# Joined high and low operands in the last group of a two-layer kernel's split products

## The chip, the core and the metric

The kernel runs on one core of a Trainium2 chip. The metric is the device time of one execution in microseconds (us), of which three runs were taken. TensorE (PE) multiplies, VectorE (DVE) and ScalarE (ACT) work on the operands and results, GpSimd (POOL) helps at the start, and SyncE (SP) issues the transfers (DMAs) one after the other.

## The reference

Sigmoid attention feeds a two-layer network with a squared ReLU:

```python
scores = scale * np.matmul(q, k.transpose(0, 1, 3, 2)) - np.log(S)
attn_out = np.matmul(1.0 / (1.0 + np.exp(-scores)), v)
x = np.ascontiguousarray(attn_out.transpose(0, 2, 1, 3)).reshape(B * S, H * D)
h = x @ w_in
r = np.maximum(h, 0.0)
return ((r * r) @ w_out).astype(np.float32)
```

q, k and v are 8 × 12 × 448 × 64, so x has 3584 rows (tokens) and 768 columns; w_in is 768 × 2048 and w_out 2048 × 768. All is float32.

## The kernel before

The kernel computes attention first and then the two weight products in four groups of tokens, `GROUPS = ((0, 512), (1024, 512), (2048, 512), (3072, 256))`. A group (g = 0 to 3) is two blocks of T tokens, so the last, g = 3, has T = 256 where the others have 512. Only this last group concerns us.

**Seven products.** Each of the two matrix products is cut in 2 × 2 blocks and computed by a scheme of Strassen's kind: 7 products of blocks, named 1 to 7, from sums and differences of operand blocks, and sums of the results. **High and low parts.** Each operand is split in a high part (the value cast to fp32r, by ScalarE, L349) and a low part (the rest, a subtraction on VectorE, L351), and each product is three matmuls: high·high, high·low, low·high (`product`, L561). A matmul has 128 rows of weights and T columns.

**First product** (`gemm1`, L569). i runs over 8 slices of the hidden columns. A step (n, i) is product n for slice i: 3 slices of the contraction times 3 matmuls, 9 in all. The steps run in a list: (1,i), (5,i−1), (2,i), (6,i), (3,i−1), (7,i), (4,i−1). Products 1, 6, 5 and 3 accumulate in PSUM bank `ha`, 7 and 4 in `hb`, 2 in `hc`. After 1, 6 and 5 ScalarE copies the bank (`snap`, L607: tiles s1, s2, s4, L609), and TensorE goes on accumulating in it only after that: (6,i) waits for s1, (5,i) for s2, (3,i) for s4. VectorE adds banks and snaps to the blocks g11, g22, g21 (L627, L633, L642), and ScalarE makes g12 from the bank (L636, Relu). j counts pairs of i; when a pair is complete, `squares` makes relu(h)² of 512 columns at once, on VectorE for 11, 22 and 21 (L592), on ScalarE for 12 (L590).

**Weights of the first product** come in four kinds: w1A (products 1 and 2), w1B (6 and 7), w1C (5 and 3), w1D (4). `load_weights` (L228) takes a buffer of a pool of 7 wide ones, shared with the weights w2 of the second product, and the load waits until TensorE is done with the buffer's last user. SP issues all loads in one order, so a load that waits holds back those behind it.

**Order.** Most steps of `gemm1` are ordered by a scheduler when the program is built. The last ten, (1,7), (5,6), (2,7), (6,7), (3,6), (7,7), (5,7), (4,6), (3,7), (4,7), with the first loads of the second product, run under `manual_schedule` (L666 to L683) in the order in which they are written. The list `work` says behind which of the ten a load (`load`, `load_last`), a split (`halve`) or an operand stands.

**Second product** (`gemm2`, L687): order 1, 2, 6, 7, 5, 4, 3; for each product 4 values of j, with one w2 tile `w2_3_n_j` and one operand each, both split, and 72 matmuls. While product n runs, the operands and weights of the next are prepared. Results are in banks oa, ob, oc; `snap` (L734) copies, `put` (L718) adds on VectorE or copies on ScalarE, and a DMA writes the output.

## Time and profile before

| | us |
|---|---|
| median of three runs | 1058.42 |
| lowest and highest run | 1058.36 and 1059.52 |
| profiled execution | 1058.8 |
| its span (first to last instruction) | 1057.0 |
| last group, first product | 59.96 |
| last group, second product | 61.78 |

The profile is of one execution, whose own time is 1058.8 us; 1.8 us lie around its span. Times in the views are from the start of the span. PE is TensorE's matmuls and PEld its weight loads, which overlap. A row of matmuls names the bank, the operand and the weights with buffer numbers left out, so `ha<-xht,w1C` is a matmul of some (5,i) or (3,i). A duration of one matmul is longer than the distance to the next, since they overlap.

### The profile page before, as it was taken

To read this page: it belongs to the slowest core of one execution; us is meant where nothing else is said; L and a number is where in the kernel's file an instruction comes from. 1 tells how busy PE (TensorE), PEld (TensorE's weight loads), DVE (VectorE), ACT (ScalarE), POOL (GpSimd) and SP (SyncE) were. 2 spreads that over 40 slices of the span, in tenths; PEclk is the share of its full clock that TensorE was granted. 3 is DMA by queue.
4 is the path that set the end of the run, shared out by engine and by line. 5 is a ranking of instruction groups with operands and counts; after the bars stand their busy time and mean duration, and the time that the engine had idled before them with its cause. 6 is when DMAs were issued, how large, how long until landed. Compare 5 with 4: busy or idle time off the path is not lost.

```text
span 1057.0 us, 16721 instructions
## 1 busy us (share of the span) xinstructions
PE 1052.7 (100%) x6433; PEld 825.5 (78%) x6433; DVE 798.7 (76%) x1009; ACT 650.8 (62%) x910; POOL 72.4 (7%) x42
## 2 busy tenths in 40 slices
PE   9999999999999999999999999999999999999998
PEld 4555555557888888888888888888888888899998
DVE  5999999996776699854555899655555998457896
ACT  7989999986766765534333757244334765255763
POOL 1322232210121000000000000000000000000000
PEclk9999999999999999999999999999999999999999
DMA  9988999964665335544332446443334344456664
GB/s 355 394 301 313 378 396 330 364 236 139 198 214 162 105 112 192 172 125 117 100 88 87 118 131 209 144 136 89 90 103 112 105 150 134 150 162 195 190 201 123
DMA packets 90832, 196.13 MB, mean 186 GB/s; under 512 B 8320, under 2 KB 51712, under 8 KB 90752
## 3 DMA queue, kind: packets, MB, share of 16 engines
q1 hardware_dynamic: 90608, 195.00, 56.6%
q8 instruction: 50, 0.82, 0.3%
q14 instruction: 30, 0.25, 0.1%
q10 hardware_dynamic: 144, 0.07, 0.0%
HBM read 154.14 MB, written 40.89 MB: 185 GB/s over the span
## 4 chain that ended last, share of the span: by engine, by line
PE 99%; DMA 0%; ACT 0%; issue 0%; DVE 0%; ACTq 0%
PE oa L565 22%; PE ha L565 22%; PE ob L565 11%; PE hb L565 11%; PE pav L313 11%; PE sc L282 9%; PE oc L565 5%; PE hc L565 5%; PE sr L298 2%; PE pav L325 2%; DMA w1C<-w 0%; PE warm_ps L791 0%; ACT w1C L349 0%; ACT o L727 0%; ACT s L609 0%
## 5 line engine op out<-in xcount | busy, mean ns | idle before, releaser
L349 ACT CAST w<-w 128x768 fp32r<-128x768 f32 x112 | 92.5, 835 | 91.4 <-DMA w<-w 86.8
L351 DVE TENSOR_TENSOR w<-w 128x768 fp32r<-128x768 f32 x112 | 106.4, 952 | 26.7 <-ACT w L349 26.3
L270 ACT ACTIVATE at<-sc 128x896 f32<-128x896 f32 x144 | 119.3, 942 | 4.1 <-PE sc L282 4.1
L609 ACT COPY s<-ha 128x512 f32<-128x512 f32 (+1 forms) x96 | 51.0, 532 | 110.7 <-PE ha L565 106.8
L313 PE MATMUL pav<-at,v 64*64 64x448 f32 x1152 | 118.1, 540 | 0.0
L313 PEld LDWEIGHTS pav<-at,v 64*64 64x64 f32 x1152 | 41.9, 133 | 60.6 <-issue 53.6
L351 DVE TENSOR_TENSOR w1A<-w1A 128x768 fp32r<-128x768 f32 x31 | 29.7, 957 | 60.6 <-ACT w1A L349 59.4
L519 DVE TENSOR_TENSOR ql<-x,qh 128x896 fp32r<-128x896 f32 x47 | 72.4, 1580 | 0.0
L166 POOL TENSOR_TENSOR a<-a,f 128x768 int32<-128x768 int32 x26 | 58.2, 2238 | 160.1 <-DVE a L163 105.7
L565 PE MATMUL oa<-o_0h,w 128*128 128x512 f32 (+1 forms) x192 | 55.7, 362 | 0.0
L565 PE MATMUL oa<-o_1h,w 128*128 128x512 f32 (+1 forms) x192 | 55.5, 362 | 0.0
L565 PE MATMUL oa<-o_2h,w 128*128 128x512 f32 (+1 forms) x192 | 55.5, 362 | 0.0
L565 PE MATMUL oa<-o_3h,w 128*128 128x512 f32 (+1 forms) x192 | 55.5, 362 | 0.0
L349 ACT CAST w1A<-w1A 128x768 fp32r<-128x768 f32 x32 | 26.7, 834 | 45.1 <-DMA w1A<-w 45.1
L282 PE MATMUL sc<-qh 64*128 64x448 f32 x282 | 54.2, 380 | 0.0
L282 PE MATMUL sc<-ql,qh 64*128 64x448 f32 x282 | 51.6, 361 | 0.0
L282 PE MATMUL sc<-qh,ql 64*128 64x448 f32 x282 | 51.6, 361 | 0.0
L351 DVE TENSOR_TENSOR w1B<-w1B 128x768 fp32r<-128x768 f32 x31 | 30.6, 988 | 25.1 <-ACT w1B L349 25.1
L351 DVE TENSOR_TENSOR w1C<-w1C 128x768 fp32r<-128x768 f32 x32 | 30.7, 960 | 18.7 <-ACT w1C L349 18.6
L592 DVE SCALAR_TENSOR_TENSOR g<-g 128x1024 f32<-128x1024 f32 (+1 forms) x40 | 42.6, 1064 | 1.2
L349 ACT CAST w1B<-w1B 128x768 fp32r<-128x768 f32 x32 | 26.7, 835 | 25.5 <-DMA w1B<-w 25.1
L349 ACT CAST w1C<-w1C 128x768 fp32r<-128x768 f32 x32 | 26.7, 833 | 25.4 <-DMA w1C<-w 25.4
(189 smaller groups left out, 2815.6 us busy)
## 6 DMA issues: line engine op xcount, KB each, us to landing
w<-w SPq DMA_DIRECT2D x112, 384.0 KB, 3.4
x<-qk SPq DMA_DIRECT2D x47, 448.0 KB, 6.6
f<-w_in SPq DMA_DIRECT2D x16, 768.0 KB, 8.9
w1A<-w SPq DMA_DIRECT2D x32, 384.0 KB, 3.1
w1B<-w SPq DMA_DIRECT2D x32, 384.0 KB, 3.3
w1C<-w SPq DMA_DIRECT2D x32, 384.0 KB, 3.4
v<-v SPq DMA_DIRECT2D x24, 448.0 KB, 7.5
w<-s SPq DMA_DIRECT2D x26, 384.0 KB, 7.9
```

Of the source, the lines that this page charges most:

```text
L166: nc.gpsimd.tensor_tensor(out=wb, in0=wb, in1=t.bitcast(I32)[:, :, 0], op=ALU.add)
L270: nc.scalar.activation(at, sc, AF.Sigmoid, bias=NEG_LOG_S, scale=SCALE)
L282: nc.tensor.matmul(sc[:, j], x[kp][rows, 1, ks], x[qp][rows, 0], start=(n == 0), stop=(n == len(passes) - 1),)
L298: nc.tensor.matmul(sc[r * KR : (r + 1) * KR, j], x[rows, 1, NT * P :], x[rows, 0], start=True, stop=True)
L313: nc.tensor.matmul(sums[columns, h], vt[rows, n % 2 * NT + t, columns], at[t][rows, j], start=(t == 0 and (n % 2, h) != (1, 1)), stop=(t = ...
L325: nc.tensor.matmul(sums[r][columns, r], vt[rows, 2 * NT, columns], rest[rows, j], start=(r == 1), stop=(r == 0))
L349: nc.scalar.copy(out=hi, in_=raw)
L351: nc.vector.tensor_sub(out=lo, in0=raw, in1=hi.bitcast(F32))
L519: nc.vector.tensor_sub(out=xs[n][1], in0=x[n], in1=xs[n][0].bitcast(F32))
L565: nc.tensor.matmul(out, a[:, c], b, start=first and n == 0, stop=last and n == 2, skip_group_check=True)
L592: nc.vector.scalar_tensor_tensor(out=t, in0=t, scalar=0.0, in1=t, op0=ALU.max, op1=ALU.mult)
L609: nc.scalar.copy(out=s, in_=banks["a", i])
```

## The change

It touches the last group only (`joined` is set where 2T is at most 512).

- **Joined operands.** High and low part of an operand lie side by side in one tile (`operand_of`, and `make` for x). In products 2, 7 and 4 of the first and 6, 7, 5 and 4 of the second, high·high and high·low become one matmul of 512 columns over both, and low·high one of 256. The bank then holds two halves.
- **Sums.** `total` adds a half and a snap, then the other half: two VectorE adds of 256 columns instead of one. In the second product snaps 6 and 7 are 512 wide, a snap 5 is new, and the sums of 22 and 21 are one add of 512 and one of 256 columns. For 12, two VectorE adds of 128 columns stand in place of ScalarE's copies.
- **Shared buffers.** Blocks 11 and 12 share a tile (g1), 22 and 21 another (g2).
- **w1D** has buffers of its own (L243 of the kernel after), not of the wide pool.
- **First weights of the second product** (w2_3_1_j) have buffers of their own too, and are loaded and split among the steps of the first product (`early`).
- **Squares** of blocks 22 and 21 are by ScalarE (Relu, then Square), except the last pair's; they are issued at the end of the step that follows the block's last sum (`flush`).

```diff
     def load_w1(g, i, kind):
         ns = KINDS[kind]
         at = min(PLACE[0][n] for n in ns)
-        return load_weights(w1[i][:, at : at + len(ns)], f"w1{kind}_{g}_{i}")
+        name = f"w1{kind}_{g}_{i}"
+        src = w1[i][:, at : at + len(ns)]
+        if kind == "D" and g == NG - 1:
+            t = op2(name, F32R, NS)
+            hi, lo = t[:, 0:1, :HALF], t[:, 1:2, :HALF]
+            nc.sync.dma_start(out=lo.bitcast(F32), in_=src)
+            return hi, lo
+        return load_weights(src, name)
...
+            else:
+                x = op2(f"xj{n}_{g}", F32R, 2 * T)
+                kind, at = SPOT[product]
+                if kind not in ys:
+                    ys[kind] = op2(f"yj{kind}_{g}", F32R, 2 * T)
+                y = ys[kind][:, at]
+                (h2, l2), (h1, l1) = ((t[..., :T], t[..., T:]) for t in (x, y))
+                ops[product] = [(h2[:, c], l2[:, c], x[:, c]) for c in range(2)] + [(h1, l1, y)]
...
     def load_w2(g, n, j):
         blocks_of = w2.rearrange("i p n c -> n p i c")[PLACE[1][n]]
-        return load_weights(blocks_of[:, 2 * j : 2 * j + 2], f"w2_{g}_{n}_{j}")
+        src, name = blocks_of[:, 2 * j : 2 * j + 2], f"w2_{g}_{n}_{j}"
+        if g == NG - 1 and n == 1:
+            hi, lo = (op2(f"{name}{c}", F32R, NS)[:, :, :HALF] for c in "hl")
+            nc.sync.dma_start(out=lo.bitcast(F32), in_=src)
+            return hi, lo
+        return load_weights(src, name)
...
-    def product(out, w, c, x, first, last):
+    def product(out, w, c, x, first, last, both=None):
 
         (wh, wl), (xh, xl) = w, x
+        if both is not None:
+            nc.tensor.matmul(out, wh[:, c], both, start=first, stop=last, skip_group_check=True)
+            nc.tensor.matmul(
+                out[:, : xh.shape[-1]], wl[:, c], xh, start=False, stop=last, skip_group_check=True
+            )
+            return
...
+    def operand_of(g, raw, name):
+        T = GROUPS[g][1]
+        if 2 * T > NS:
+            return (*split(raw, name, lambda *names: op2(*names, T)), None)
+        both = op2(name, F32R, 2 * T)
+        hi, lo = both[:, :, :T], both[:, :, T:]
+        split_to(hi, lo, raw)
+        return hi, lo, both
+
...
+        joined = (2, 7, 4) if 2 * T <= NS else ()
...
+            j = i // 2
+            if (n, j) not in blocks:
+                if 2 * T > NS:
+                    blocks[n, j] = op2(f"g{n}_{g}_{j}", n=T)
+                else:
+                    t = op2(f"g{n[0]}_{g}_{j}", n=2 * T)
+                    for k, c in enumerate("12"):
+                        blocks[n[0] + c, j] = t[:, k].rearrange("p (a s) -> p a s", a=2)
+            return blocks[n, j][:, i % 2]
...
-            if g == 0:
+            if g == 0 or (g == NG - 1 and i < NI - 2):
                 pending.append(lambda: squares(n, i, scalar=True))
             else:
                 squares(n, i)
...
+        def total(to, from_, s):
+            nc.vector.tensor_add(out=to, in0=from_[:, :T], in1=s)
+            if joined:
+                nc.vector.tensor_add(out=to, in0=from_[:, T:], in1=to)
...
             for c in range(NE):
-                product(out, w, c, ops[n][c], n in (1, 7, 2) and c == 0, c == NE - 1)
+                *x, both = ops[n][c]
+                product(out, w, c, x, n in (1, 7, 2) and c == 0, c == NE - 1, both if n in joined else None)
...
-                nc.vector.tensor_add(out=tile_of("11", i), in0=out, in1=snaps[1, i])
+                total(tile_of("11", i), out, snaps[1, i])
...
-                nc.vector.tensor_add(out=tile_of("22", i), in0=banks["b", i], in1=snaps[4, i])
+                total(tile_of("22", i), banks["b", i], snaps[4, i])
                 squares_later("22", i)
...
-                nc.vector.tensor_add(out=tile_of("21", i), in0=out, in1=snaps[2, i])
+                total(tile_of("21", i), out, snaps[2, i])
                 squares_later("21", i)
...
-            operands[j] = split(blocks["11", j], f"o1_{g}_{j}", lambda *name: op2(*name, T))
+            operands[j] = operand_of(g, blocks["11", j], f"o1_{g}_{j}")
...
+        early = {}
+        if g == NG - 1:
+            for j in range(NI // 2):
+                early[30 + 3 * j] = lambda j=j: load(j)
+                early[35 + 3 * j] = lambda j=j: halve(j)
         for at, (n, i) in enumerate(head):
             run(n, i)
             for work in between.get(at, ()):
                 work()
+            if at in early:
+                early[at]()
...
+        work = [(at, piece, arg) for at, piece, arg in work if not (early and piece in (load, halve))]
...
+        joined = (6, 7, 5, 4) if 2 * T <= NS else ()
...
-            ops.setdefault(n, {})[j] = split(raw, f"o{n}_{g}_{j}", new)
+            ops.setdefault(n, {})[j] = operand_of(g, raw, f"o{n}_{g}_{j}")
...
-            if add is not None:
-                nc.vector.tensor_add(out=o, in0=banks[k, e], in1=snaps[add, e])
-            elif g == NG - 1 and e == NE - 1:
-
+            if name == "11":
+                nc.vector.tensor_add(out=o, in0=banks[k, e], in1=s)
+            elif joined and name == "12":
                 for columns, queue in ((slice(0, T // 2), nc.sync), (slice(T // 2, T), nc.scalar)):
-                    nc.scalar.copy(out=o[:, columns], in_=banks[k, e][:, columns])
-                    queue.dma_start(out=to[:, columns], in_=o[:, columns])
-                return
+                    nc.vector.tensor_add(out=o[:, columns], in0=banks[k, e][:, columns], in1=s[:, columns])
+                    if e == NE - 1:
+                        queue.dma_start(out=to[:, columns], in_=o[:, columns])
+                if e == NE - 1:
+                    return
+            elif joined:
+                nc.vector.tensor_add(out=s, in0=banks[k, e], in1=s)
+                nc.vector.tensor_add(out=o, in0=s[:, :T], in1=s[:, T:])
+            elif add is not None:
+                nc.vector.tensor_add(out=o, in0=banks[k, e], in1=s)
             else:
                 nc.scalar.copy(out=o, in_=banks[k, e])
             nc.sync.dma_start(out=to, in_=o)
...
-            s = snaps[n, e] = op1(f"t{n}_{g}_{e}", n=T)
-            nc.scalar.copy(out=s, in_=banks[k, e])
+            from_ = banks[k, e][:, {1: slice(T), 5: slice(T, 2 * T)}.get(n, slice(None))]
+            s = snaps[n, e] = op1(f"t{n}_{g}_{e}", n=from_.shape[-1])
+            nc.scalar.copy(out=s, in_=from_)
...
-                    banks[k, e] = bank(f"o{k}_{g}_{e}")[:, :T]
+                    banks[k, e] = bank(f"o{k}_{g}_{e}")[:, : (2 if joined and n != 2 else 1) * T]
...
-                        x = tuple(t[:, i % 2] for t in ops[n][j])
-                        product(banks[k, e], w, e, x, n in (1, 7, 2) and i == 0, i == NI - 1)
+                        x, both = tuple(t[:, i % 2] for t in ops[n][j][:2]), None
+                        to = banks[k, e][:, :T]
+                        if n in joined:
+                            both, to = ops[n][j][2][:, i % 2], banks[k, e]
+                        product(to, w, e, x, n in (1, 7, 2) and i == 0, i == NI - 1, both)
...
+                    if joined:
+                        snap(5, k, e)
                     put("22", e, 1, 7)
                 elif n == 3:
-                    put("12", e, 1, None)
+                    put("12", e, 1, 5 if joined else None)
```

**Where instructions move.** Names in these rows: `w1D_3_5` is the weights of kind D, group 3, i = 5, `s4_3_6` the snap after (5,6), `w2_3_2_2` the weights of product 2, j = 2, in the second product, `g2_3_2` the shared tile of blocks 22 and 21, j = 2 (i = 4 and 5); the last number counts tiles.

TensorE near the end of the first product, before: the last of (7,6), then (4,5), which is `hb_3_5` with w1D_3_5, then the first of (1,7).

```order
L565 MATMUL hb_3_6_8935<-xht3_3_8271,w1B_3_6_8908 128x256
L565 MATMUL hb_3_6_8935<-yt3_3_8273,w1B_3_6_8908 128x256 x3
L565 MATMUL hb_3_5_8838<-xht4_3_8407,w1D_3_5_8945 128x256
L565 MATMUL hb_3_5_8838<-xlt4_3_8408,w1D_3_5_8945 128x256
L565 MATMUL hb_3_5_8838<-xht4_3_8407,w1D_3_5_8945 128x256 x2
L565 MATMUL hb_3_5_8838<-xlt4_3_8408,w1D_3_5_8945 128x256
L565 MATMUL hb_3_5_8838<-xht4_3_8407,w1D_3_5_8945 128x256
L565 MATMUL hb_3_5_8838<-yt4_3_8409,w1D_3_5_8945 128x256 x3
L565 MATMUL ha_3_7_8978<-xh11_3_8137,w1A_3_7_8960 128x256
```

And after: the last of (2,7), then (6,7), (4,5) and the first of (3,6), which is `ha_3_6` with w1C_3_6.

```order
L588 MATMUL hc_3_7_8975<-yjA_3_8138,w1A_3_7_8927 128x256
L593 MATMUL ha_3_7_8945<-xjt2_3_8223,w1B_3_7_8935 128x256 x6
L593 MATMUL ha_3_7_8945<-yjB_3_8224,w1B_3_7_8935 128x256 x3
L587 MATMUL hb_3_5_8808<-xjt4_3_8394,w1D_3_5_8915 128x512
L588 MATMUL hb_3_5_8808<-xjt4_3_8394,w1D_3_5_8915 128x256
L587 MATMUL hb_3_5_8808<-xjt4_3_8394,w1D_3_5_8915 128x512
L588 MATMUL hb_3_5_8808<-xjt4_3_8394,w1D_3_5_8915 128x256
L587 MATMUL hb_3_5_8808<-yjD_3_8395,w1D_3_5_8915 128x512
L588 MATMUL hb_3_5_8808<-yjD_3_8395,w1D_3_5_8915 128x256
L593 MATMUL ha_3_6_8833<-xj22_3_8346,w1C_3_6_8931 128x256 x6
```

The step (4,5) has moved from behind (7,6) to behind (6,7), past (1,7), (5,6) and (2,7); (3,6) comes right after it.

SP at the same place, before: the loads from w1C of i = 5 on.

```order
L232 DMA w1C_3_5_8879<-w1 128x768
L232 DMA w1B_3_6_8908<-w1 128x768
L232 DMA w1D_3_5_8945<-w1 128x384
L232 DMA w1A_3_7_8960<-w1 128x768
L232 DMA w1C_3_6_8964<-w1 128x768
L232 DMA w1B_3_7_8968<-w1 128x768
L232 DMA w1D_3_6_8972<-w1 128x384
L232 DMA w1C_3_7_8990<-w1 128x768
```

And after, from w1C of i = 7 to the first weights of product 6.

```order
L232 DMA w1C_3_7_8959<-w1 128x768
L232 DMA w2_3_2_0_9081<-w2 128x2x384
L232 DMA w2_3_2_1_9106<-w2 128x2x384
L232 DMA w2_3_2_2_9131<-w2 128x2x384
L243 DMA w1D_3_5_8915<-w1 128x384
L243 DMA w1D_3_6_8939<-w1 128x384
L232 DMA w2_3_2_3_9156<-w2 128x2x384
L243 DMA w1D_3_7_8998<-w1 128x384
L232 DMA w2_3_6_0_9192<-w2 128x2x384
```

The loads w1D_3_5 and w1D_3_6 have moved behind the loads of w1C_3_7 and of w2_3_2_0 to w2_3_2_2, each of which waits for a wide buffer; w2_3_2_2 takes the one of w1B_3_6.

ScalarE at the same place, before: the snaps of (1,7), (5,6) and (6,7) and what follows.

```order
L609 COPY s1_3_7_8988<-ha_3_7_8978 128x256
L609 COPY s4_3_6_9001<-ha_3_6_8867 128x256
L609 COPY s2_3_7_9028<-ha_3_7_8978 128x256
L349 CAST w1C_3_7_8990<-w1C_3_7_8990 128x768
L636 ACTIVATE g12_3_3_9043<-ha_3_6_8867 128x256
L349 CAST w2_3_1_0_9017<-w2_3_1_0_9017 128x768
L609 COPY s4_3_7_9068<-ha_3_7_8978 128x256
```

And after, from the snap of (1,7) to that of (5,7).

```order
L653 COPY s1_3_7_8955<-ha_3_7_8945 128x256
L356 CAST w2_3_2_1_9106<-w2_3_2_1_9106 128x768
L356 CAST w2_3_2_2_9131<-w2_3_2_2_9131 128x768
L356 CAST w1D_3_5_8915<-w1D_3_5_8915 128x384
L356 CAST w1D_3_6_8939<-w1D_3_6_8939 128x384
L356 CAST w2_3_2_3_9156<-w2_3_2_3_9156 128x768
L633 ACTIVATE g2_3_2_8762<-g2_3_2_8762 128x512
L634 ACTIVATE g2_3_2_8762<-g2_3_2_8762 128x512
L653 COPY s4_3_6_8970<-ha_3_6_8833 128x256
L653 COPY s2_3_7_8994<-ha_3_7_8945 128x256
L356 CAST w1C_3_7_8959<-w1C_3_7_8959 128x768
L686 ACTIVATE g1_3_3_8872<-ha_3_6_8833 128x256
L356 CAST w2_3_6_0_9192<-w2_3_6_0_9192 128x768
L653 COPY s4_3_7_9026<-ha_3_7_8945 128x256
```

The snap s4_3_6 stood behind s1_3_7; now five casts of weights and the Relu and Square of g2_3_2 stand between them.

## Rows read from the trace of the kernel before

**Rows 1.** From the page: busy time (share of span) and count by engine; granted clock in 40 slices

```profile
PE 1052.7 (100%) x6433; PEld 825.5 (78%) x6433; DVE 798.7 (76%) x1009; ACT 650.8 (62%) x910; POOL 72.4 (7%) x42
...
PEclk9999999999999999999999999999999999999999
```

**Rows 2.** Busy by stretch (first, second product): us, PE, PEld, DVE, ACT, POOL, clock

```profile
932.22:992.18 59.96, 59.90 (x498) 59.69 (x497) 40.72 (x68) 33.81 (x68) 0.00 (x0) 1.00 0.61 183
992.18:1053.96 61.78, 61.77 (x513) 61.39 (x512) 52.90 (x81) 39.37 (x66) 0.00 (x0) 1.00 0.60 174
```

**Rows 3.** Waits of TensorE's queue, 925 to 1058: us in all, times, longest

```profile
PEld ha L565 <- ACT s L609: 0.3, 1, 0.3
PEld hb L565 <- DVE w1D L351: 0.2, 1, 0.2
```

**Rows 4.** The chain that ended last, 925 to 1058: start, us, what

```profile
958.38 4.19 DMA w1C<-w
...
962.65 0.83 ACT w1C L349
963.48 0.28 ACT s L609
```

**Rows 5.** Timeline of TensorE, 512 columns, the group ahead: start, us, instruction

```profile
924.28 0.39 PE L565 MATMUL oa<-o_2l,w 128*128 128x512 f32 x1
...
927.68 0.39 PE L565 MATMUL oa<-o_2l,w 128*128 128x512 f32 x1
```

**Rows 6.** Timeline of TensorE, 256 columns, first product of the last group

```profile
960.35 0.28 PE L565 MATMUL ha<-xht,w1C 128*128 128x256 f32 x1
...
962.51 0.28 PE L565 MATMUL ha<-xht,w1B 128*128 128x256 f32 x1
```

**Rows 7.** VectorE by line and form, 932.3 to 1054: count | busy us, mean ns | idle before

```profile
L351 DVE TENSOR_TENSOR w<-w 128x768 fp32r<-128x768 f32 x28 | 26.6, 951 | 1.3 <-ACT w L349 1.2
L592 DVE SCALAR_TENSOR_TENSOR g<-g 128x512 f32<-128x512 f32 x12 | 8.3, 688 | 0.2
...
L351 DVE TENSOR_TENSOR w1D<-w1D 128x384 fp32r<-128x384 f32 x7 | 3.9, 552 | 0.0
L642 DVE TENSOR_TENSOR g<-hb,s 128x256 f32<-128x256 f32 x8 | 3.4, 420 | 1.5 <-PE hb L565 1.5
```

**Rows 8.** ScalarE by line and form, 932.3 to 1054

```profile
L609 ACT COPY s<-ha 128x256 f32<-128x256 f32 x24 | 8.7, 369 | 5.9 <-PE ha L565 5.9
...
L349 ACT CAST w1D<-w1D 128x384 fp32r<-128x384 f32 x7 | 3.6, 509 | 0.0
...
L590 ACT ACTIVATE g<-g 128x512 f32<-128x512 f32 x4 | 2.5, 630 | 0.0
```

**Rows 9.** DMA issues, 930 to 1058: count, KB each, median us to landing

```profile
w<-w SPq DMA_DIRECT2D x28, 384.0 KB, 3.6
w1C<-w SPq DMA_DIRECT2D x7, 384.0 KB, 3.7
...
w1D<-w SPq DMA_DIRECT2D x7, 192.0 KB, 2.3
```

**Rows 10.** Timeline of SP's issues, 981 to 983

```profile
981.37 0.37 SPq L232 DMA_DIRECT2D w<-w  x1
982.45 0.32 SPq L232 DMA_DIRECT2D w1D<-w  x1
```

**Rows 11.** DMA issues of 981 to 982, 982 to 983, 985.6 to 986

```profile
w<-w SPq DMA_DIRECT2D x1, 384.0 KB, 3.9
...
w1D<-w SPq DMA_DIRECT2D x1, 192.0 KB, 3.2
...
w<-w SPq DMA_DIRECT2D x1, 384.0 KB, 3.1
```

**Rows 12.** Timeline of ScalarE, three casts in a row

```profile
995.15 2.30 ACT L349 CAST w<-w 128x768 fp32r<-128x768 f32 x3
```

**Rows 13.** End of the chain that ended last

```profile
1054.19 0.27 ACT o L727
```

More of the change, by code (lines that the diff above doesn't have):

```diff
@@ L379, in sub @@
                 nc.vector.tensor_sub(out=o, in0=x, in1=y)
-        ops = {}
+        ops, ys = {}, {}
         def make(product, n, later=None):
-            h2, l2, both = (op2(f"{c}{n}_{g}", F32R, T) for c in ("xh", "xl", "y"))
-            h1, l1 = both[:, 0], both[:, 1]
-            ops[product] = [(h2[:, 0], l2[:, 0]), (h2[:, 1], l2[:, 1]), (h1, l1)]
+            if 2 * T > NS:
+                y = op2(f"y{n}_{g}", F32R, T)
+                h1, l1 = y[:, 0], y[:, 1]
+                h2, l2 = (op2(f"{c}{n}_{g}", F32R, T) for c in ("xh", "xl"))
+                ops[product] = [(h2[:, c], l2[:, c], None) for c in range(2)] + [(h1, l1, None)]
+            else:
[6 more added lines that the diff above has]
+                ops[product] = [(h2[:, c], l2[:, c], x[:, c]) for c in range(2)] + [(h1, l1, y)]
             for x, (hi, lo) in zip(raw[n], [(h2, l2), (h1, l1)]):
@@ L578, in tile_of @@
         def tile_of(n, i):
-            if (n, i // 2) not in blocks:
-                blocks[n, i // 2] = op2(f"g{n}_{g}_{i // 2}", n=T)
-            return blocks[n, i // 2][:, i % 2]
+            j = i // 2
+            if (n, j) not in blocks:
+                if 2 * T > NS:
+                    blocks[n, j] = op2(f"g{n}_{g}_{j}", n=T)
[4 more added lines that the diff above has]
+            return blocks[n, j][:, i % 2]
         def squares(n, i, scalar=False):
@@ L617, in run @@
             if n in (1, 7, 2):
-                banks[k, i] = bank(f"h{k}_{g}_{i}")[:, :T]
+                banks[k, i] = bank(f"h{k}_{g}_{i}")[:, : (2 if n in joined else 1) * T]
             out = banks[k, i]
@@ L691, in gemm2 @@
         t2 = {}
-        def new(name, dtype):
-            return op2(name, dtype, T)
+        joined = (6, 7, 5, 4) if 2 * T <= NS else ()
         def operand(n, j):
@@ L698, in operand @@
                 if j not in operands1:
-                    operands1[j] = split(blocks["11", j], f"o1_{g}_{j}", new)
+                    operands1[j] = operand_of(g, blocks["11", j], f"o1_{g}_{j}")
                 if j not in weights1:
@@ L720, in put @@
             o = op1(f"o{name}_{g}_{e}", n=T)
+            s = snaps.get((add, e))
             to = outT[(r + e) * P : (r + e + 1) * P, t0 + b * T : t0 + (b + 1) * T]
-            if add is not None:
-                nc.vector.tensor_add(out=o, in0=banks[k, e], in1=snaps[add, e])
-            elif g == NG - 1 and e == NE - 1:
+            if name == "11":
+                nc.vector.tensor_add(out=o, in0=banks[k, e], in1=s)
+            elif joined and name == "12":
                 for columns, queue in ((slice(0, T // 2), nc.sync), (slice(T // 2, T), nc.scalar)):
-                    nc.scalar.copy(out=o[:, columns], in_=banks[k, e][:, columns])
-                    queue.dma_start(out=to[:, columns], in_=o[:, columns])
-                return
+                    nc.vector.tensor_add(out=o[:, columns], in0=banks[k, e][:, columns], in1=s[:, columns])
[8 more added lines that the diff above has]
+                nc.vector.tensor_add(out=o, in0=banks[k, e], in1=s)
             else:
```

## The prediction

> **What bounds the kernel now.** I read four views in this order. First, the page: TensorE is busy for all of the span at full clock, VectorE for 76% of it [rows 1]. So time can be won only by giving TensorE less to do, and is lost wherever TensorE has to wait. Second, the busy times of the two products of the last group, the only stretch that the change touches [rows 2]: the first product lasts 59.96 us, the second 61.78 us, together 121.74 us. They hold 1008 matmuls of 256 columns, and 1008 × 0.120 us (the pitch, below) is 120.96 us. TensorE hardly waits there, while VectorE has 19 us and 9 us free and ScalarE more. Third, the waits of TensorE's queue in the last group [rows 3]: two, 0.3 us for a ScalarE copy and 0.2 us for the low part of w1D. Fourth, the chain that ended last [rows 4], which shows how the first arises: a weight load (w1C) landed late, its cast stood ahead of the snap on ScalarE, and TensorE waited for the snap. That pattern, an instruction that waits for a transfer with a snap queued behind it, is the one to look for in the new order.
>
> **What the joining removes.** Three matmuls of 256 columns (high·high, high·low, low·high) become one of 512 and one of 256 columns. The columns stay the same; only one instruction's fixed part goes. From pitches: 15 matmuls of 512 columns start from 924.28 up to 927.68 [rows 5], so 3.40/15 = 0.2267 us; 18 of 256 columns from 960.35 up to 962.51 [rows 6], 2.16/18 = 0.120 us. Three of 0.120 are 0.360 us, one of each is 0.3467 us: 0.0133 us saved a triple. Per product of the first stage there are 3 such triples, 3 products and 8 values of i: 72. In the second, 4 products of 24 triples: 96. So 168 triples, 168 × 0.0133 = **2.24 us** gained, all on TensorE.
>
> The Trainium skill, page "TensorE: Matmul & The Clock Gate", section "Back-to-back issue gap", speaks against this: by its isolated gap of N/2.4 + 2.5 ns only 2.5 ns are fixed in a matmul, an estimate of 168 × 2.5 ns = 0.42 us for the gain, and a sum of 1064.4 below. The trace disagrees (227 ns at 512 columns where that formula gives 216, 120 at 256 where it gives 109) and decides.
>
> **What the joining adds** is work of VectorE, since the halves of a bank must be summed: 24 more adds of 256 columns in the first product, against 6 squares of 512 columns that go to ScalarE. By [rows 7], 24 × 0.42 − 6 × 0.69 = +5.9 us, to about 46.6 of 60 us. In the second, the end sums get a few adds longer and the 4 splits of the first weights (4 × 0.95) move ahead, so its 52.9 us hardly change. ScalarE gets 6 times Relu and Square, 12 × 0.63 = 7.6 us [rows 8], on 33.8 of 60 us. Neither engine becomes the bound on average: these cost nothing by themselves, covered by TensorE's matmuls. If that cover were gone, the first stage alone would owe up to 5.9 us. What costs is where they stand in a queue. The wait of 0.3 us of [rows 3] goes, since kinds A, B and C now have the seven wide buffers alone: −0.3 us.
>
> **The new wait at the end of the first product.** The order shows: (4,5) has moved from right behind (7,6) to behind (6,7), four products later, and its weights, w1D of i=5, are issued on SP behind w2_3_2_2, which waits for the buffer that (7,6) frees. On ScalarE the cast of w1D_3_5 stands behind that of w2_3_2_2; then come Relu and Square of a block that contains (4,5)'s own sums; and behind these s4_3_6, the snap that (3,6) waits for. Before, s4_3_6 ran right behind its product (a copy of 0.37 us [rows 8]), and (4,5) followed (7,6) without a wait.
>
> Walk, with t = 0 at the end of (7,6). (1,7), (5,6), (6,7) take 1.08 us each and the joined (2,7) 1.04: TensorE wants (4,5) at 4.28. Transfers: a w load takes 3.6 us from issue to landing at the median [rows 9], so w2_3_2_2 lands at 3.65. In the trace a w issued at 981.37 took 3.9 us and a w1D behind it at 982.45 took 3.2 us [rows 10, 11], so it landed 0.4 us after; w1D_3_5 is there at 4.1. Casts: ScalarE starts 0.1 us after a landing [rows 4], and three casts of 768 columns take 2.30 us [rows 12], one alone 0.83 [rows 4], so one starts 0.73 after the other; w2_3_2_2 runs 3.75 to 4.49, w1D_3_5 (0.51 us [rows 8]) to 5.0. TensorE starts at 5.05, a wait of 0.77. Its second matmul needs the low part: VectorE subtracts w2_3_2_2 (0.95 us) from 4.63 to 5.5, then w1D_3_5 (0.55 [rows 7]) to 6.05, each again starting a little before the recorded end of the one ahead; TensorE goes on at 6.1, a second wait of 0.8. The sums of (4,5) come out at 7.07, VectorE's two adds end at 7.86, Relu at 8.42, Square at 8.94, s4_3_6 at 9.31, and (3,6) starts at 9.36 instead of 5.32: **4.0 us** lost. Bounds: 3.1 us if the transfers land as a w on a quiet queue does (3.1 [rows 11]), 4.3 us if w2_3_2_2 takes 3.9.
>
> **Waits that follow it.** (a) VectorE reaches the low part of w1C_3_7 behind the adds and the square that waited for s4_3_6, so (5,7) waits about 0.5 us. The snap s4_3_7 for (3,7) stands behind the cast of w2_3_6_0, whose buffer is free only at the end of (3,6): 0.05 + 3.1 + 0.1 + 0.84 + 0.37 + 0.05 = 4.5 us later (3.1 the landing), while (7,7), (5,7) with its wait, and (4,6) cover 3.7: another 0.8. Together 1.25 us, between 1.0 and 1.6. (b) w1D of i = 1, 2 and 3 now has a buffer of its own, but SP issues it right behind a w1C that waits for one, and (4,i) follows four products later. For i = 2, from the end of (2,3), which frees the buffer of w1C_3_4: TensorE does (6,3), (3,2), (7,3), (1,4) and a matmul of (5,3) and is at (4,2) at 4.4; w1C lands at 3.75 (3.7 us from its issue [rows 9]), w1D 0.4 later, ScalarE casts the one from 3.85 to 4.58 and the other to 5.1: 0.7 us of wait. For i = 1 ScalarE casts w1D first, and 0.45 is left; for i = 3, 0.1: together 1.25. The nearest row is the wait of 0.2 us for w1D [rows 3]; if only that and as little beside it show, the end is 0.3; with each w1D 0.25 later it is 2.0. I take the walk, made of measured durations. (c) The start of the second product: ScalarE and VectorE are behind by the waits above, 0.2 us (0 to 0.5). (d) The end: two adds of 128 columns instead of ScalarE copies after the last matmul. Before, ScalarE's copy takes 0.27 us of the chain [rows 13]; the adds are on one engine, the second DMA on another: +0.1 (−0.1 to 0.2).
>
> The early loads of w2_3_1 cost nothing: they take the place of w1D transfers that end sooner, ScalarE has room; they take 4 of the 28 transfers of the second stage away, and the rest are one product ahead as before.
>
> **The sum.** −2.24 − 0.3 + 4.0 + 1.25 + 1.25 + 0.2 + 0.1 = +4.26 us. The profiled execution took 1058.8 us (span 1057.0, 1.8 around it); with the change 1063.0. The median is 1058.42, 0.4 less; so I predict **1062.6 us**. With the bounds, gain 2.5 and waits 4.4 to 8.6, the case's own range is 1060.3 to 1064.5.
>
> **Rivals.** *Half hidden.* If w1D_3_5 landed before 3.6 us, its cast (0.51) would end before TensorE comes at 4.28, and if VectorE were ahead too, (4,5) would run at once. For it: a w1D lands in 2.3 us at the median [rows 9]. Against it: SP issues in order, and the w ahead of it waits for (7,6). The first wait would shrink to what stands between the end of (4,5) and s4_3_6 in any case (two adds, Relu, Square, copy: 9.36 − 6.9, about 2.4 us), and those of (a) to (c) to between nothing and 2: 1058.4 − 2.54 + 2.4 + (0 to 2) = 1058.3 to 1060.3, no change. *The joining hides more.* If a matmul of 512 columns covered the weight load behind it wholly, a triple would save two fixed parts, 26.6 ns, and the 168 of them 4.5 us. For it: weight loads are busy for 78% of the span [rows 1], and a triple has one less. Against it: matmuls of 512 columns in the group ahead show the same fixed part of 13 ns as those of 256 [rows 5, 6]. It decides from a pitch of the pair under 0.335 us. With the waits half hidden it gives 1058.4 − 4.5 − 0.3 + 2.4 = 1056.0, faster; with my waits, 1060.3. *VectorE becomes the bound in the second product.* Before, it is busy 52.9 of 61.8 us [rows 2]; after, about 60.5 us are left to TensorE, and a product's operands are prepared during the one ahead. It decides where VectorE's share there passes 95%; then the six adds of 512 columns that the change puts into the sums of 22 and 21 come on top, 6 × 0.69 = 4.1 us: 1066.7, slower.
>
> **How the numbers follow.** The forecast (late w1D, snaps behind ScalarE's squares) gets 0.76; half hidden, with the joining that hides more under my waits, 0.12; joining and hidden waits together, 0.07; VectorE as the bound, 0.05. The range leaves out the last two, part of the half-hidden case and the far end of mine: 1059.3 to 1064.6. What a measurement can tell from no change is 0.2%, 2.1 us: 1056.3 to 1060.5. So faster 0.07, same 0.14 (0.12 and the low end of the forecast), slower 0.79.
>
> **What the profile after would show.** TensorE's waits in the last group: for the cast of w1D and its low part at (4,5), together 1.6 us; for the snap s behind it, 2.4 us; then for w1C's low part and a snap, 1.25 us; and shorter ones for w1D. The chain that ended last goes from the w load through casts, (4,5), VectorE's adds, Relu, Square and the snap. The pitch of a 512 + 256 pair is 0.347 us. The second product lasts about 60.5 us, 1.28 less (96 × 13.3 ns), with no wait in its middle. Wrong would be: no wait above 1 us at (3,6); a pitch of the pair under 0.34 or over 0.36; VectorE without gaps in the second product.

## The result, and the profile after

The changed kernel takes 1068.22 us (median of five runs, 1067.60 to 1068.67) beside 1058.66 us for the one before (five runs): a ratio of 1.0089, with a 95% interval of 1.0074 to 1.0104. It is slower, as forecast, but by 9.6 us and not by 4.2. The profiled execution took 1068.26 us with a span of 1066.5, 9.5 more than before. Of e5, below, one run took 1168.09 us at a granted clock of 0.85; its time is the median of the other ten.

All of that lies in the last group. The two stretches, cut where the second product starts (columns as in [rows 2]; the last two are the busy share of the DMA and its GB/s), are 69.34 and 62.26 us long, where they were 59.96 and 61.78. VectorE is not the bound of either. The clock of the first is 0.95, where it was 1.00:

```profile
931.92:1001.26 69.34, 63.13 (x427) 57.36 (x426) 50.85 (x89) 45.40 (x87) 0.00 (x0) 0.95 0.61 190
1001.26:1063.52 62.26, 61.48 (x416) 56.24 (x414) 53.33 (x87) 35.27 (x60) 0.00 (x0) 1.00 0.46 134
```

The waits of TensorE's queue, first from 935 to 982 us, then from 982 to 1066 us; before there were two, of 0.5 us together [rows 3]:

```profile
PEld hb L587 <- ACT w1D L356: 1.6, 4, 0.6
PEld hb L588 <- DVE w1D L358: 0.9, 2, 0.7
...
PEld ha L593 <- ACT s L653: 3.9, 2, 3.1
PEld hb L587 <- ACT w1D L356: 1.7, 1, 1.7
PEld oa L593 <- DVE o L358: 1.1, 1, 1.1
PEld hb L588 <- DVE w1D L358: 0.9, 1, 0.9
```

They are waits of the forecast, each where it was put: for the cast and the low part of w1D at (4,5), for s4_3_6 at (3,6), for s4_3_7 at (3,7), and shorter ones for w1D before; the one of 0.5 us forecast for (5,7) did not come, and the last, of 1.1 us at the start of the second product, was forecast at 0.2. The chain that ended last goes through the walk of the prediction, step by step, as [rows 4] did for the short wait of before:

```profile
982.82 4.41 DMA w<-w
987.26 0.84 ACT w L356
...
988.99 0.56 DVE w1D L358
989.60 0.39 PE hb L588
...
990.90 0.44 DVE g L656
991.36 0.43 DVE g L658
991.81 0.64 ACT g L633
992.48 0.63 ACT g L634
993.11 0.27 ACT s L653
993.42 2.30 PE ha L593 x9
995.74 3.19 DMA w<-w
998.94 0.84 ACT w L356
...
1002.95 0.74 PE oa L593 x4
```

(7,6) ends at 982.8; the load of w2_3_2_2 starts there, w1D_3_5 is cast and split behind it, (4,5) runs, its sums pass VectorE, Relu and Square, and the snap lets (3,6) start at 993.42, 10.6 us after (7,6) where the walk said 9.4. Then comes something that the forecast had not: nine matmuls take 2.30 us. The timeline of TensorE there:

```profile
986.56 0.52 PE L593 MATMUL ha<-yjB,w1B 128*128 128x256 f32 x3
988.55 0.49 PE L587 MATMUL hb<-xjt,w1D 128*128 128x512 f32 x1 [1.48 <-ACT w1D L356]
989.60 0.39 PE L588 MATMUL hb<-xjt,w1D 128*128 128x256 f32 x1 [0.55 <-DVE w1D L358]
...
993.42 1.65 PE L593 MATMUL ha<-xj,w1C 128*128 128x256 f32 x6 [2.56 <-ACT s L653]
994.87 0.84 PE L593 MATMUL ha<-yjC,w1C 128*128 128x256 f32 x3
995.50 0.63 PE L587 MATMUL hb<-xjt,w1B 128*128 128x512 f32 x1
...
997.32 0.88 PE L593 MATMUL ha<-xjt,w1C 128*128 128x256 f32 x6
```

Six matmuls start over 1.45 us (993.42 to 994.87), 0.24 each, twice the pitch of [rows 6]. (3,6) takes 2.08 us where nine times 0.120 is 1.08, and (7,7) 1.82 where three pairs of 0.353 are 1.06: 1.76 us. The granted clock explains it (busy times by stretch, the clock third from the end):

```profile
986.00:990.00 4.00, 1.97 (x13) 1.46 (x12) 2.79 (x4) 1.84 (x4) 0.00 (x0) 1.00 0.73 225
990.00:993.00 3.00, 0.86 (x4) 0.32 (x3) 1.73 (x4) 1.81 (x3) 0.00 (x0) 0.56 0.04 13
993.00:997.00 4.00, 3.58 (x14) 3.39 (x15) 3.17 (x6) 1.75 (x5) 0.00 (x0) 0.50 0.07 8
997.00:1000.00 3.00, 2.61 (x17) 2.12 (x16) 0.19 (x1) 1.06 (x3) 0.00 (x0) 0.97 0.75 223
```

After a stretch with TensorE busy for 1.97 of 4 us, it falls to 0.50, the 1.2 GHz level, stays there through the first 3.7 us of full work, and is back at 2.4 GHz from about 997.2. It falls at 990.3 (finer stretches have 1.00 up to 990.30 and 0.50 from 990.40): behind the waits for w1D, and ahead of the long one for s4_3_6.

The gain is smaller too. In the second product a 512-column and a 256-column matmul alternate:

```profile
1022.20 0.40 PE L587 MATMUL oa<-o,w 128*128 128x512 f32 x1
1022.44 0.28 PE L588 MATMUL oa<-o,w 128*128 128x256 f32 x1
...
1025.38 0.40 PE L587 MATMUL oa<-o,w 128*128 128x512 f32 x1
```

Nine pairs in 3.18 us are 0.3533 us a pair, not 0.3467 as the pitches of [rows 5, 6] give one by one. That is 6.7 ns saved on three times 0.120, half of the forecast: 168 × 6.7 ns = 1.1 us.

### The profile page after: what moved, and what is told of

Read it like the earlier page. It is cut to its first block, busy times and chain, and to the rows that moved or that the text cites. A ratio compares the mean times of both kernels' runs of the same rounds, so it can differ in the third digit from the quotient of the medians.

```text
span 1066.5 us, 16387 instructions
## 1 busy us (share of the span) xinstructions
PE 1054.9 (99%) x6265; PEld 817.1 (77%) x6265; DVE 808.8 (76%) x1039; ACT 658.3 (62%) x921; POOL 72.3 (7%) x42
## 4 chain that ended last, share of the span: by engine, by line
PE 95%; DMA 2%; DVE 1%; ACT 1%; issue 0%; SPq 0%; DVEq 0%; ACTq 0%
PE ha L593 20%; PE oa L593 20%; PE pav L320 11%; PE hb L593 9%; PE ob L593 9%; PE sc L289 8%; PE oc L593 5%; PE hc L593 5%; PE pav L332 2%; PE sr L305 2%; PE oa L587 1%; PE ob L587 1%; DMA w<-w 1%; PE hb L587 1%; PE ob L588 1%; PE oa L588 1%
## 5 line engine op out<-in xcount | busy, mean ns | idle before, releaser
L356 ACT CAST w<-w 128x768 fp32r<-128x768 f32 x108 | 89.5, 836 | 97.9 <-DMA w<-w 95.7
L358 DVE TENSOR_TENSOR w<-w 128x768 fp32r<-128x768 f32 x108 | 102.9, 955 | 33.1 <-ACT w L356 32.9
L656 DVE TENSOR_TENSOR g<-hb,s 128x512 f32<-128x512 f32 (+1 forms) x64 | 39.7, 620 | 29.4 <-ACT s L653 22.4
L593 PE MATMUL oa<-o_0h,w 128*128 128x512 f32 x144 | 46.3, 389 | 0.0
L593 PE MATMUL oa<-o_1h,w 128*128 128x512 f32 x144 | 46.3, 389 | 0.0
L593 PE MATMUL oa<-o_2h,w 128*128 128x512 f32 x144 | 46.3, 389 | 0.0
L593 PE MATMUL oa<-o_3h,w 128*128 128x512 f32 x144 | 46.3, 389 | 0.0
```

The source lines that it names most:

```text
L356: nc.scalar.copy(out=hi, in_=raw)
L358: nc.vector.tensor_sub(out=lo, in0=raw, in1=hi.bitcast(F32))
L593: nc.tensor.matmul(out, a[:, c], b, start=first and n == 0, stop=last and n == 2, skip_group_check=True)
L656: nc.vector.tensor_add(out=to, in0=from_[:, :T], in1=s)
```

## The experiments

e1 to e12 were timed beside the kernel before on the same chip (its medians there: 1058.2 to 1058.4 us); the times are medians of 4 to 11 runs. "Joining" stands for the joined operands with their sums.

| kernel | what it has of the change | us | ratio to before (95%) |
|---|---|---|---|
| changed | all | 1068.22 | 1.0089 (1.0074 to 1.0104) |
| e1 | all, TensorE kept busy in the two long waits | 1067.59 | 1.0086 (1.0072 to 1.0100) |
| e2 | all, one pair fewer squared by ScalarE | 1064.73 | 1.0057 (1.0043 to 1.0071) |
| e3 | all but w1D's own buffers | 1061.56 | 1.0029 (1.0018 to 1.0041) |
| e4 | all, w1D loaded earlier | 1062.07 | 1.0037 (1.0025 to 1.0050) |
| e5 | joining alone | 1059.25 | 1.0010 (1.0001 to 1.0019) |
| e6 | all but the early first weights | 1062.17 | 1.0040 (1.0027 to 1.0052) |
| e7 | all but the joining | 1061.39 | 1.0032 (1.0020 to 1.0043) |
| e8 | joining and early first weights | 1061.06 | 1.0032 (1.0020 to 1.0044) |
| e9 | as e8, second weights placed by hand | 1059.08 | 1.0008 (0.9999 to 1.0016) |
| e10 | as e9, short matmul into the other half | 1059.25 | 1.0008 (0.9999 to 1.0017) |
| e11 | as e9, joining in the second product alone | 1057.82 | 0.9996 (0.9987 to 1.0005) |
| e12 | as e11, long and short matmuls grouped | 1057.55 | 0.9992 (0.9983 to 1.0002) |

### e1: is it the clock?

```diff
-            if n in (1, 7, 2):
+            if n in (1, 7, 2) and (k, i) not in banks:
...
+            if g == NG - 1 and (n, i) == (3, NI - 2):
+                spare = banks["b", NI - 1] = bank(f"hb_{g}_{NI - 1}")
+                for m in range(24):
+                    nc.tensor.matmul(
+                        spare[:, :T], weights[NI - 1, "B"][0][:, 0, :P], ops[6][0][0], start=True, stop=True, skip_group_check=True
+                    )
```

> The changed kernel with 24 extra matmuls of 256 columns put where TensorE waits for w1D_3_5 and for s4_3_6 (2, 6 and 16 of them; their results are overwritten by (7,7) and used by nothing). The transfers, casts and sums and their order stay, so the snap comes as late as before. Theory (the late snap idles TensorE, its clock falls to 1.2 GHz, and (3,6) and (7,7) then run at half speed): the clock stays at 1.00 through 990 to 997 us of the span, the nine matmuls of (3,6) take 1.08 us instead of 2.08 and (7,7) 1.04 instead of 1.82, and the time falls from 1068.2 by 1.8 to about 1066.4. Rival (what is slow behind the wait is not the clock but late operands): the time stays within 0.4 of 1068.2.

The clock stayed at 1.00 and (3,6) ran at full speed, from 993.41 where it was 993.42. The time fell by only 0.6 us (0.4 when each kernel is taken beside its own runs of before: 9.2 and 9.6 us above). The timeline, and below it two steps of the chain that ended last, say where the rest went:

```profile
990.69 2.07 PE L671 MATMUL hb<-xjt,w1B 128*128 128x256 f32 x16
993.41 0.98 PE L593 MATMUL ha<-xj,w1C 128*128 128x256 f32 x6 [0.66 <-ACT s L653]
...
995.64 0.40 PE L593 MATMUL ha<-xjt,w1C 128*128 128x256 f32 x2
996.72 0.74 PE L593 MATMUL ha<-xjt,w1C 128*128 128x256 f32 x4 [0.67 <-DVE w1C L358]
```

```profile
994.78 3.34 DMA w<-w
...
1002.14 0.74 PE oa L593 x4
```

With full clock (5,7) is reached earlier and waits for the low part of w1C_3_7, the wait of 0.5 us in the forecast, which the slow clock had covered. What is left comes from (3,6), whose end lets the load of w2_3_6_0 start: it starts at 994.78 and not at 995.74, and TensorE gets its operand in the second product at 1002.14 and not at 1002.95, 0.8 us earlier in these two executions. So the clock is the cause of the slow matmuls, as expected, but of 1.76 us lost to it less than 1 is on the path: the price that I expected, 1.8, was wrong, and 0.4 to 0.6 us between medians are about as much as such a comparison can tell.

### e2, e3, e4: the queue ahead of the snap, and late w1D

```diff
-            if g == 0 or (g == NG - 1 and i < NI - 2):
+            if g == 0 or (g == NG - 1 and i < NI - 4):
```

> The changed kernel with one pair fewer squared by ScalarE: blocks 22 and 21 of j = 2 go back to VectorE, so no Relu and Square stand ahead of s4_3_6. The scheduler then also puts (4,5) three products earlier. Theory (the loss at the end of the first product is the queue ahead of s4_3_6 and the clock behind it): the wait for s4_3_6 of 2.9 us and the slow clock (1.85) go, the waits for w1D stay: about 1068.2 - 2.9 - 1.8 = 1063.5, or 1061 if the wait of 2.5 at (4,5) shrinks too. Rival (the joining itself costs, by its sums on VectorE): still above 1066.

```diff
-        if kind == "D" and g == NG - 1:
+        if False:
```

> The changed kernel with w1D loaded into the wide pool again, everything else as changed, the squares by ScalarE too. (4,5) is then again right behind (7,6). Theory (late w1D is the root): all waits for w1D (2.4 us at i = 0 to 3, 2.5 at i = 5) go, the Relu and Square run earlier and s4_3_6 is in time: 1056.3 to 1058.0. Rival (ScalarE's squares are the cause by themselves): the snaps s stay late, 1061 or more.

```diff
             kind, at = SPOT[n]
+            if g == NG - 1 and n == 5 and (i, "D") not in weights and i < NI - 1:
+                weights[i, "D"] = halve_weights(load_w1(g, i, "D"))
```

> The changed kernel with each w1D of i = 0 to 6 loaded and split at (5,i), two or three products ahead of the step that uses it, in its own buffers as changed. The Relu and Square of j = 2 still stand ahead of s4_3_6 in ScalarE's order, but (4,5), whose sums they take, is again right behind (7,6). Theory (the place of the w1D loads is what matters, not their buffers): 1056.3 to 1058.5, no wait above 0.5 us. Rival (Relu and Square ahead of the snap cost wherever (4,5) stands): a wait for s4_3_6 of over 1 us stays, 1060 or more.

e2 came out 3.5 us below the changed kernel, nearer to the theory: s4_3_6 was in time, but w1C's low part (1.7 us) and s4_3_7 (1.6 us) were late in its place. Since (4,5) moved as well, e2 does not price the squares alone. e3 and e4 were 6.7 and 6.2 us below, so most of the loss needs the late w1D; but both stay 3 to 4 us above before, more than I had expected: the rivals' times came. The waits of TensorE's queue, e3 first, then e4:

```profile
PEld ha L593 <- DVE w1C L358: 1.8, 1, 1.8
PEld ha L593 <- ACT s L653: 1.6, 1, 1.6
PEld oa L593 <- DVE o L358: 0.6, 1, 0.6
```

```profile
PEld ha L593 <- ACT s L653: 4.7, 4, 2.8
PEld oa L593 <- DVE o L358: 1.1, 1, 1.1
```

The waits for w1D are gone in both, and s4_3_6 is late all the same. ScalarE's timeline of e4 shows by what:

```profile
984.86 0.36 ACT L653 COPY s<-ha 128x256 f32<-128x256 f32 x1
987.12 0.83 ACT L356 CAST w<-w 128x768 fp32r<-128x768 f32 x1 [1.90 <-DMA w<-w]
987.86 0.62 ACT L633 ACTIVATE g<-g 128x512 f32<-128x512 f32 x1
988.52 0.63 ACT L634 ACTIVATE g<-g 128x512 f32<-128x512 f32 x1
989.05 0.63 ACT L653 COPY s<-ha 128x256 f32<-128x256 f32 x2
```

ScalarE waits 1.90 us for a transfer of w2_3_2 before a cast that nobody needs yet, and Relu, Square and the snap wait behind it. So there is a second cause that does not need w1D: casts of the second product's next weights, hoisted ahead of the last snaps. Relu and Square, the rivals' reason, have their share: they take 1.2 of the 1.9 us from the start of this cast to the snap. e4 also tells of the clock: the profiled execution, in which it fell, took 1064.17 us, and the four in which it stayed at 1.00 took 1061.54 to 1062.12. It is one execution, and 2 us there stand beside less than 1 in e1, so one price for the clock does not follow.

### e5 to e8: part by part

```diff
-            if g == 0 or (g == NG - 1 and i < NI - 2):
+            if g == 0:
...
-        if kind == "D" and g == NG - 1:
+        if False:
...
-        if g == NG - 1 and n == 1:
+        if False:
...
-        if g == NG - 1:
+        if False:
             for j in range(NI // 2):
```

> The joined operands with their sums and the shared block buffers alone: squares by VectorE, w1D in the wide pool, the first weights of the second product loaded in the tail, all three as in the kernel before. The order of the steps is that of before, with s4_3_6 right behind s1_3_7. Theory (the joining gives its 2.24 us, the loss is all in the other three parts): 1056.2, between 1055.6 and 1056.9, no wait above 0.5 us. Rival (the joining's own sums and 512-column snaps cost what it saves): 1058 or more, with waits for VectorE's sums.

e6 has only the last two of these edits, e8 the first two.

> The changed kernel with the first weights of the second product in the wide pool and in the tail as before; w1D in its own buffers and ScalarE's squares as changed. In the tail, two casts of w2 and the transfers that they wait for then no longer stand ahead of s4_3_6 and w1C_3_7, but Relu and Square of j = 2 do. Theory (casts of w2 that wait for their buffer ahead of a snap are the larger part of the loss at the end; with w1D in its own buffers its waits of about 2.4 us stay): 1059 to 1061. Rival (the early loads are free, late w1D and the squares are all of it): 1064 or more.

```diff
-        joined = (2, 7, 4) if 2 * T <= NS else ()
+        joined = ()
...
-        joined = (6, 7, 5, 4) if 2 * T <= NS else ()
+        joined = ()
```

> The changed kernel without the joining: three matmuls of 256 columns everywhere and one add for a sum, but w1D's own buffers, the early first weights, ScalarE's squares and the shared blocks as changed. Theory (the waits come from these and not from the joining): 2.24 us more matmul time and nearly the same waits, 1066 to 1070. Rival (VectorE's 24 more adds make w1D and w1C late): 1062 or less.

> The joining with the early first weights alone; w1D in the wide pool and squares by VectorE as before. s4_3_6 is again right behind s1_3_7, but the casts of w2_3_2_1 and w2_3_2_2 stand ahead of s4_3_7 on ScalarE, and of the sums of (5,7) on VectorE. Theory (an early load of the one product's weights lets the next product's, which must wait for a buffer, go ahead of the last snaps): a wait of 1 to 2 us for s4_3_7 or for the operand behind it, 1057.3 to 1058.5. Rival (early loads are free): as the joining alone, 1056.2.

e5, the joining alone, is 1.1 us slower than before, so the rival held: the sums eat what the joining gives. Its second stretch has VectorE at 59.44 of 63 us, and TensorE waits for two things:

```profile
991.00:1054.00 63.00, 61.97 (x421) 56.91 (x419) 59.44 (x94) 41.66 (x68) 0.00 (x0) 1.00 0.57 171
```

```profile
PEld oa L593 <- DVE o L358: 1.4, 2, 1.2
PEld ha L593 <- ACT s L653: 0.9, 3, 0.5
```

The longest wait, 1.2 us, is for the low part of an operand in the second product, until 999.46: around 990 to 1000 us VectorE does the last sums, squares and the splits of the first weights in a row, with three more adds than before. That the adds push the low part back is read from this order; e9, below, has the same sums but the splits behind the operands, and waits 0.2 us for operands, and the kernel before, with the splits and without the adds, has no such wait [rows 3]: it takes both. e6 is 1062.17, a little above its forecast of 1059 to 1061: without the early weights the waits for w1D (2.3 us) stay, and those of 1.4 us for operands of the second product are as in e5. e8 is 1061.06, above the forecast too: TensorE waits 1.4 us each for snaps and for w1C's low part, and 1.1 for an operand. It is 1.8 us above e5, and that is what the early first weights cost here. e7 refuted my theory, that the waits have nothing to do with the joining: 1061.39, the rival's number, with 2.3 us of waits in all. But the rival's reason is only half of it: the other three parts without the joining cost 3.2 us, the joining alone 1.1, and all together 9.6. The order shows what couples them: in e7 and e2 the scheduler puts w1D_3_5 behind w2_3_2_0, in the changed kernel behind w2_3_2_2, and (4,5) two to three products later. So the long wait is not in one part, but in the order that comes out of all four: taking away w1D's buffers, the early weights or the joining gives back 6 to 7 us each. No run kept all four parts and moved only the next weights, so that the order by itself gives all of it back is not shown, nor why the scheduler's choice tips there.

### e9 to e12: what the joining is worth when nothing waits

e9 is e8 with this:

```diff
-        work = [(at, piece, arg) for at, piece, arg in work if not (early and piece in (load, halve))]
+        if early:
+            work = [(at, {load: load_next, halve: halve_next}.get(piece, piece), arg) for at, piece, arg in work]
+            work.sort(key=lambda item: (item[0], item[1] is halve_next))
```

`load_next` and `halve_next` load and split w2_3_2_j, and the second product takes these tiles (lines left out here).

> The joining with the early first weights; w1D in the wide pool and squares by VectorE as before; and the second weights (w2_3_2_j) loaded and split at the places of the tail where the kernel before has the first ones, so that none of their casts stands ahead of s4_3_6, and only w2_3_2_0 ahead of s4_3_7, as w2_3_1_0 did before. Measured so far: a joined pair takes 0.3533 us, so the joining gives 168 x 6.7 ns = 1.1 us. Theory (the waits of e8 come from the hoisted casts, those of e5 from the first weights' splits on VectorE at the start of the second product): both go, 1056.8 to 1057.6. Rival (VectorE's added sums are the bound there in any case): a wait of 1 us for an operand stays, 1058.5 or more.

e10 adds one edit, e11 another instead:

```diff
-                out[:, : xh.shape[-1]], wl[:, c], xh, start=False, stop=last, skip_group_check=True
+                out[:, xh.shape[-1] :], wl[:, c], xh, start=False, stop=last, skip_group_check=True
...
-        joined = (2, 7, 4) if 2 * T <= NS else ()
+        joined = ()
```

> As e9, but the matmul of 256 columns (low x high) adds to the upper half of the bank instead of the lower; the halves are summed in the end, so the sum is the same. Theory (the pair takes 0.3533 us and not 0.3467 because the short matmul adds to the columns that the long one has just written first): the pair at 0.3467 us, 1.1 us less than e9. Rival (the extra 6.7 ns come from the change of length or weights and not from the place): 0.3533 us, within 0.3 us of e9.

> As e9, with the joining in the second product alone; the first has three matmuls of 256 columns and one add for a sum. Theory (72 pairs less give back 0.48 us, VectorE has 24 adds less in the first product): 0.4 us above e9 if e9 has no waits, and below e9 by what its waits in the first product are: 1057.2 to 1057.8. Rival (the sums in the first product cost more than the joining there gives): below e9 by 0.5 or more.

```diff
-                for e in range(NE):
+                for part, e in itertools.product((0, 1) if n in joined else (None,), range(NE)):
```

Part 0 is the matmul of 512 columns, part 1 the short one (the lines that pass the part on are left out).

> As e11, but within each j of a joined product of the second stage the six matmuls of 512 columns run first and then the six of 256, so that the length (and high and low weights) change twice in twelve matmuls and not each time. Theory (the extra 6.7 ns a pair belong to a short matmul followed by a long one or back): 512 to 512 at 0.2267 and 256 to 256 at 0.120 us, so 96 x 6.7 ns x 5/6 = 0.5 us less than e11: 1057.3 beside a before of 1058.4. Rival (they belong to the 512-column matmul over two parts of an operand): a pair stays at 0.353 us and the time within 0.2 us of e11.

e9 is 2.0 us below e8: the hoisted casts were that. It still has waits of 1.6 us, nearly all in the first product (for a snap and for w1C's low part), so it is 0.7 us above before (the interval just includes no change) and not below. e10 has the same pair of 0.353 us: the place in the bank is not what makes the pair slower. e11 gives up the joining in the first product and has two waits of 0.2 us each; it is 1.3 us below e9, so there the sums did cost more than the joining gave. e12 shows what grouping does to TensorE's pitch:

```profile
1014.60 1.55 PE L588 MATMUL oa<-o,w 128*128 128x512 f32 x6
1015.99 0.88 PE L590 MATMUL oa<-o,w 128*128 128x256 f32 x6
1016.70 1.55 PE L588 MATMUL oa<-o,w 128*128 128x512 f32 x6
```

Six of 512 columns in 1.39 us and six of 256 in 0.71 are 0.350 us a pair, 3.3 ns below 0.3533: half of the extra 6.7 ns is the alternation, half stays. What stays is in the long matmuls: 0.232 us each here, where the group ahead has 0.2267. e12 is 0.3 us below e11, which the runs cannot tell apart. Both are 0.5 to 0.7 us below before, with intervals that just include no change (to 1.0005 and 1.0002): a version that surely beats before was not found.

## Why the prediction was right and wrong

The direction and the mechanism were right: a transfer late by SP's order, a cast that waits for it, and the snap behind Relu and Square. The size was wrong, 9.6 instead of 4.2 us. What failed are terms of the sum: the slow clock had none, the early loads and VectorE's added sums were put at nothing, and the gain, the transfer ahead of (4,5), w1D before i = 5 and the start of the second product were sized wrong. By its steps:

| term | predicted | measured |
|---|---|---|
| 168 joined triples | −2.24 | −1.1 |
| (4,5) waits for w1D_3_5 | 0.77 + 0.8 | 1.7 + 0.9 |
| (3,6) waits for s4_3_6 | 2.4 | 3.1 |
| slow clock behind it | none | 1.8 |
| (5,7) and (3,7) | 1.25 | 0.8 |
| w1D before i = 5 | 1.25 | 2.5 |
| start of the second product | 0.2 | 1.1 |
| the two waits of before | −0.3 | −0.5 |
| the end | 0.1 | −0.1 |

The right column sums to 10.2, the span grew by 9.5. The waits are read from the queue of weight loads, which else run a little ahead, so a wait there (1.7, 0.9, 3.1 us) is longer than the gap that it leaves between matmuls (1.6, 0.8, 2.9 by the starts in the timeline): 0.4 us. The other 0.3 lie ahead of the group, whose first product starts at 931.92 where it was 932.22.

**The joining's gain** was sized from pitches of unmixed runs [rows 5, 6]. Mixed, a pair takes 6.7 ns more. The rival of a gain of 4.5 us went the other way. The Trainium skill's isolated gap ("TensorE: Matmul & The Clock Gate", "Back-to-back issue gap") gives an estimate of 216 + 109 = 325 ns for the pair, and the trace has 353.

**The transfer ahead of (4,5).** I took 3.6 us, the median of [rows 9], for w2_3_2_2; it took 4.4, and the two w1D behind it 4.5 each (DMA issues from 982.5 to 983 and from 983.2 to 983.9 us):

```profile
w<-w SPq DMA_DIRECT2D x1, 384.0 KB, 4.4
...
w1D<-w SPq DMA_DIRECT2D x2, 192.0 KB, 4.5
```

Four loads were issued within 2.4 us there (981.77 to 984.2); the bound of 3.9 came from two in flight [rows 10, 11] and was too low. This is 0.8 us of the term.

**The clock** had no term. It stood at 1.00 all through the profile of before, and I had not asked what the new waits do to it. The matmuls lost 1.76 us to it; e1 puts 0.4 to 0.8 of that on the path, since the rest ran beside other waits.

**w1D before i = 5.** i = 0 was costed at nothing; it waits 0.7 us for its low part, and the walk's slack for i = 3 was too wide.

**The start of the second product** was sized at 0.2 us as a mere delay. It is a chain of its own: s4_3_7, behind the cast of w2_3_6_0, holds back VectorE's sums, square and the operand o1. e8 has the same wait, and in e9, with the casts of the next weights at places by hand, 0.2 us are left of it.

**The early loads and the sums** were put at nothing, the sums as covered by TensorE's matmuls. The early loads cost 1.8 us (e8 beside e5), because the next weights then go ahead of the last snaps; without them the changed kernel would be 6 us faster (e6). The sums of the first product cost 1.3 us more than the joining gives there (e9 beside e11): they are not covered.

**The rivals.** Half hidden was too mild, VectorE as the bound of the second product did not come (53.33 of 62.26 us), and the second product itself lost nothing in its middle, as forecast (62.26 us, where about 60.5 were forecast, are half of the gain and the wait at its start).

## What to carry to other kernels

On an engine that runs in order, look for each instruction that waits for a transfer and ask who stands behind it: a cast of weights needed a product later can hold a snap that the matmuls need now, and a scheduler puts it there as soon as a buffer is free. Changes that free buffers move such work forward, so they want the same hand-written places as what they replace. And a saving per instruction is to be measured in the mix in which it will run, with the engine that pays for it followed to the place where it has no slack.

## What the hardware showed that was not expected

A 512-column matmul in a stream with 256-column ones takes more than alone: a pair 0.3533 us against 0.2267 + 0.120; grouped in sixes 0.350. Neither the half of the bank (e10) nor the alternation alone (e12) explains it; the rest, 5 ns more in a long matmul than in the group ahead, stays open. TensorE's granted clock fell to 0.50 after 986 to 990 us with half of the time idle and came back some 3.7 us after full work had begun; of the loss of 1.76 us in the matmuls, 0.4 to 0.8 us were in the kernel's time (e1).
